# Attention and gated FFN on one core: k-v products moved into the runs of the batch before, remainder pairs two at a time

## The chip, the cores and the metric

The kernel runs on one core of a Trainium2 chip. A core has TensorE (PE), VectorE (DVE), ScalarE (ACT), GpSimd (POOL) and SyncE (SP), each with an instruction stream of its own, worked off in order, and 16 DMA engines that all of them share. PE writes its results to PSUM, which the kernel cuts into eight tiles of 128 x 512 numbers; DVE and ACT read them from there. SP issues no arithmetic here: its stream holds DMAs alone, and an instruction of SP that waits holds up all that stand behind it. POOL has arithmetic and DMAs in one stream. The metric is the device time of one execution in microseconds (us), as the median of several.

## The reference

For 8 batches, 8 heads, 576 positions and 64 dimensions:

```python
kv = np.einsum('bhsd,bhse->bhde', k, v)
out = np.einsum('bhsd,bhde->bhse', q, kv)
rms = np.sqrt(np.mean(out * out, axis=-1, keepdims=True) + 1e-06)
attn = out / rms * g_norm
x = attn.transpose(0, 2, 1, 3).reshape(4608, 512)
rms = np.sqrt(np.mean(x * x, axis=-1, keepdims=True) + 1e-06)
xn = x / rms * rms_g
g = xn @ w_gate                      # 512 x 1536
silu = g * (1.0 / (1.0 + np.exp(-g)))
result = (silu * (xn @ w_val)) @ w_out
```

So attention has no softmax: a batch needs one 64x64 product of k and v for each head, and then q times it ("o"). Both norms are folded into one factor for each position and head.

## The kernel before

**Work and groups.** A batch's 576 positions are cut into 512 main ones, four chunks of 128, and a remainder of 64. The FFN runs over nine groups of 512 rows: the main positions of batches 0 to 6 in order, then the eight remainders together (`xr`, the group that the code calls B), then batch 7. In a group, the FFN is a row of slots: 24 for the first layer, alternately a gate (4 matmuls of 128x512, then silu on ACT) and a value (4 matmuls, then their product with silu on DVE), and 16 slots of 3 matmuls for the second layer. The attention of batch b is spread over the slots of group b-1, so that its x is there when group b starts. "Group 1" below is the stretch in which the attention of batch 2 is made, and so on; slot numbers count from the group's start.

**Who sets the order.** `Placer` (line 40) is a planner: it holds a load for each engine and slot. `put` gives an operation to the first slot from a given one in which the engine's backlog, by the costs written in the code, stays under a bound (`ROOM` lists what a slot of a kind offers, `BEHIND` what backlog is allowed; POOL has 0.85 a slot in the first layer, 0.65 in the second, and 2.0 of backlog). What is put first takes the room; what is put later goes where room is left. Instructions come out slot by slot: first the slot's operations for engines other than PE, then the FFN's matmuls of the slot, then the slot's other PE work. DMAs on SP have a cost of zero, and a landing time that the planner assumes (6 slots for q, 4 for x). The waits themselves come from semaphores that the framework adds by data; the planner sets the order alone.

**A batch's attention** (`place_attention`, line 669). (1) k and v come by POOL's DMAs, which also convert them to bf16 (`loads_kv`: k main, k remainder, v main, v remainder; two buffers of each, by the parity of the batch). (2) q comes by SP into `stg`, is converted by POOL in two halves (`main_q`), its remainder apart (`remq`, one tile for two batches), and is then transposed by SP's DMAs (`qT_dma`, line 379). (3) PE makes the k-v products: 40 matmuls of 64x64 (`kv_mm`, line 285), into a PSUM tile that two DVE copies empty (`kv_half`). (4) PE makes o, 32 matmuls (`o_heads`, line 412). (5) ACT squares and copies o, POOL weights the squares with the norm's gain, DVE sums both, works out the factor in a chain of 13 small steps and multiplies (`xna`). (6) SP transposes the result into x in two DMAs (`x_dma`, line 645). In SP's order, the transposition of the next batch's q can stand ahead of x's.

**Runs.** Steps 3 and 4 put runs of small matmuls between those of the FFN. Batches 2 and 3 have a run of k-v products each; batches 4 and 5 share one, 6 and 7 too (`mate`). Each of these runs stands in the last slots of the group before the one in which o follows; o of a batch stands behind slot 2 of its group (batch 2: slot 7).

**Remainders.** The remainders' o is made for two batches at a time (16 matmuls, `o_rem`), with the o of batch 2 (remainders of 0 and 1), 3, 5 and 7. Its two PSUM tiles, half full, are squared and copied by ACT as four halves each. It is a fifth chunk of its batch for all that follows. The products of k and v lie in three tiles `kvs`, each a block-diagonal 128x128 for two heads, two of them cleared by POOL at the start.

PSUM is split into three tiles `mm1` for the FFN's first layer, two `o2` for the second, and three `att`; o of a batch takes both `o2`, two `att`, and, with a remainder, a third `att` and an `mm1`.

Of the kernel before, what the change touches and what calls it, by code (L numbers as in the profile page):

```python
# [87 lines left out]
def kernel(  # L88
# [38 lines left out]
    xna_p = pool("xna", 2)  # L127
    x_p = pool("x", 3)
# [30 lines left out]
    q01r = consts.tile([2 * REM, H, D], BF16, name="q01r")  # L159
# [29 lines left out]
    def load_cast(b, t, heads=None):  # L189
        to = qc if t == 0 else (vc if t == 2 else kc)[b % 2]  # L190
        if heads is None:
            if t == 0:
                to = q01r[b * REM : (b + 1) * REM]
            else:
                to = to[:REM, :, NC * D :]
            return nc.gpsimd.dma_start(
                out=to, in_=src[t][b, :, MAIN:S, :].rearrange("h p d -> p h d")
            )
        view = src[t][b, :, 0:MAIN, :].rearrange("h (p c) d -> p h (c d)", c=NC)[:, heads[0] : heads[1]]
        return nc.gpsimd.dma_start(out=to[:, heads[0] : heads[1], : NC * D], in_=view)  # L200
# [62 lines left out]
    class Att:  # L263
        def __init__(self, b):
            self.b = b
            self.kv, self.qT = kvs[b % 2 if b else 2], qTs[b % 2]
            self.chunks = NC + (b == 2 or b > 2 and b % 2)
            if b < 2:
                self.qTj = self.qT.rearrange("p c j t -> p (c j t)").rearrange("p (j c t) -> p j c t", j=NS, c=NC + 1)
# [51 lines left out]

        def kv_half(self, half):
            rows, cols = slice(half * D, (half + 1) * D), slice(half * D, (half + 1) * D)
            nc.vector.tensor_copy(out=self.kv[rows, :, half, :], in_=self.kv_ps[rows, :, cols])  # L324
# [54 lines left out]
        def qT_dma(self):  # L379
            flat = mains[self.b, 0].rearrange("p c h d -> p (c h d)")  # L380
            nc.sync.dma_start_transpose(out=self.qT[:, 0:NC].rearrange("p c j t -> p (c j) t"), in_=flat)
            if self.chunks > NC:
                rem = q01r if self.b == 2 else rems[0][self.b // 2 % 2]
                nc.sync.dma_start_transpose(out=self.qT[:, NC], in_=rem.rearrange("p h d -> p (h d)"))

        def o_rem(self):

            of = (kvs[2], kvs[1]) if self.b == 2 else (kvs[0], kvs[1])
            self.o[NC] = [
                pool_.tile([128, H // 2, D], FP32, name=name) for pool_, name in ((att_p, "att"), (mm1_p, "mm1"))  # L390
            ]
            for j in range(NS):
                for n in range(2):
                    at = slice(n * REM, (n + 1) * REM)
                    for half in range(2):
                        rows = slice(half * D, (half + 1) * D)
                        nc.tensor.matmul(  # L397
                            self.o[NC][half][at, j, :], lhsT=self.qTj[rows, j, NC, at],
                            rhs=of[n][rows, j, half, :], start=True, stop=True, skip_group_check=True,
                        )  # L400

        def sq_rem(self, half):
            if NC not in self.sq:
                self.sq[NC] = sq_p.tile([128, 2, H, D], BF16, name="sq")
            nc.scalar.activation(out=self.sq[NC][:, 0, half:H:2, :], in_=self.o[NC][half], func=ACT.Square)  # L405

        def outa_rem(self, half):
            if NC not in self.outa:
                self.outa[NC] = outa_p.tile([128, H, D], BF16, name="outa")
            nc.scalar.copy(out=self.outa[NC][:, half:H:2, :], in_=self.o[NC][half])  # L410

        def o_heads(self):
# [5 lines left out]
            for c in range(NC):  # L418
                for j in range(NS):
                    for half in range(2):  # L420
# [3 lines left out]
                            rhs=self.kv[rows, j, half, :], start=True, stop=True, skip_group_check=True,  # L424
# [4 lines left out]
        def part(self, t, n):  # L429

            if n >= NC:
                return t[:, n]
# [12 lines left out]
        def xna_pairs(self, o, js, c0, c1):  # L445
            if not hasattr(self, "xna"):
                self.xna = xna_p.tile([128, NC + 1, H, D], BF16, name="xna")
# [6 lines left out]
        def o_of(self, c):  # L454
            return self.o[c] if c >= NC else self.o["main", c].rearrange("p c h d -> p (c h) d")
# [60 lines left out]
        def red(self, c, which):  # L516
            if self.st is None:
                self.st = stat.tile([128, 2, NC + 1, H], FP32, name="st")
            of = self.sq[c][:, which]
            if c < NC:  # L520
                of = of.rearrange("p (c h) d -> p c h d", c=2)
            nc.vector.reduce_sum(out=self.part(self.st[:, which], c), in_=of, axis=AX.X)  # L522

        def chain_t(self):
            if not hasattr(self, "al"):
                t = lambda n, dt=FP32, h=H: stat.tile([128, NC + 1, h], dt, name=n)
                self.u, self.r, self.t, self.z, self.nt, self.al = (t(n) for n in ("u", "r", "t", "z", "nt", "al"))
                self.s = stat.tile([128, NC + 1], FP32, name="srow")
# [57 lines left out]
        def xna_(self, c, eng):  # L586
            if not hasattr(self, "xna"):
                self.xna = xna_p.tile([128, NC + 1, H, D], BF16, name="xna")
            if c < NC:
                of = self.o["main", c] if self.b == 1 else self.outa[c].rearrange("p (c h) d -> p c h d", c=2)  # L590
                return eng.tensor_tensor(  # L591
                    out=self.part(self.xna, c), in0=of,
                    in1=self.part(self.al, c).to_broadcast([128, 2, H // 2, D]), op=OP.mult,
                )
            return eng.tensor_tensor(
                out=self.xna[:, c], in0=self.outa[c], in1=self.al[:, c, :].to_broadcast([128, H, D]), op=OP.mult
# [48 lines left out]
        def x_dma(self, c0, c1):  # L645
# [3 lines left out]
            else:  # L649
                b = self.b // 2 * 2 if self.b > 2 else 0  # L650
                to = xr[:, :, b * REM : (b + 2) * REM]
                of = self.xna[:, NC].rearrange("p h d -> p (h d)")
# [16 lines left out]
    def place_attention(P, b, casts=(), at=0, chain_at=0, mate=None):  # L669
# [3 lines left out]
        N1 = range(a.chunks)  # L673
        P.floor = max(P.floor, at)
        load = P.put("SP", 0.0, a.qT_dma, casts[:1] if b == 2 else casts)
        qt = [("DMA", load[1] + QT_SLOTS)]
        if kv is None:
            of = [a] + ([Att(mate)] if mate else [])
            p = P.psum(1.2, lambda: [o.kv_mm(ALL) for o in of], casts, len(of))
            out_ = [[P.put("DVE", 0.4, lambda o=o, h=h: o.kv_half(h), [p]) for h in range(2)] for o in of]  # L680
            for tile_, ops in zip(P.tiles[-len(of) :], out_):
                tile_ += ops
            kv = out_[0]
            if mate:
                ahead[mate] = of[1], out_[1]
        else:
            P.floor = max(P.floor, start + 2)
        outs, reds = {}, []
        rem = a.chunks - NC
        main = P.psum(0.73 + 0.25 * rem, a.o_heads, kv + qt, 2 + rem)  # L690
        for c in (*N1[NC:], *N1[:NC]):
            if c == NC:
                for n in (1, 0):
                    s = P.put("ACT", 0.38, lambda n=n: a.sq_rem(n), [main])
                    outs[c] = P.put("ACT", 0.38, lambda n=n: a.outa_rem(n), [main])
                P.tiles[-1] += [s, outs[c]]
            else:
                s = P.put("ACT", 0.6, lambda c=c: a.sq_(c), [main])
                outs[c] = P.put("ACT", 0.6, lambda c=c: a.outa_(c), [main])
                if c >= 2:  # L700
                    P.tiles[c - NC - rem] += [s, outs[c]]
            assert outs[c][1] < start + 2 * NF, (b, outs)
            w = P.put("POOL", 1.2, lambda c=c: a.wsq(c, nc.gpsimd), [s])
            reds.append(P.put("DVE", 0.68, lambda c=c: a.red(c, 0), [s]))
# [424 lines left out]
```

## Time and profile before

| | us |
|---|---|
| median of three runs | 317.73 (317.66 to 317.91) |
| the profiled execution's own time | 317.42 |
| its span, first to last instruction | 315.6 |
| PE busy | 309.0 |
| DVE, ACT, POOL busy | 167.4, 139.0, 87.3 |
| FFN matmul, start to start | 0.216 |
| a slot of the first layer, of the second | 0.86, 0.65 |
| transposing DMA of q, issue to landing (median) | 7.5 |
| of x | 3.2 |
| a load of k, of v (512 KB, median) | 7.9, 12.8 |

The span is that of the profile's instructions; the time of an execution has some 1.8 us around it. In a line of a timeline stand the start, the length, the engine, the line of the kernel, the operation, what it writes and reads, and how many were merged; the first two are in us. Matmuls overlap: one of 512 columns is listed with 0.38 us, but the next starts 0.216 after it. Some matmul records are missing, so that a count can be one or two short. A line of a DMA issue gives the time from issue to landing at its end; q0 is the queue that POOL's loads go through, q1 that of SP's DMAs, and the last figure of a queue's line is the time that its packets took, as a share of the 16 engines (over 100% where packets overlap in an engine).

### The profile page before, as it was taken

Reading aid. Unit: us, or ns where it says so; the run is one execution under the profiler, and the core shown is the slowest. Engines: PE = TensorE matmul, PEld = TensorE weight load, DVE = VectorE, ACT = ScalarE, POOL = GpSimd, SP = SyncE. Lnnn points to the kernel's source line nnn. Section 1 sums busy time; section 2 is a strip of 40 time slices with the busy share of each in tenths; the row PEclk is TensorE's granted clock in tenths of the full one; section 3 lists DMA queues with packets and bytes.
Section 4 is the critical chain, followed back from the end, with each engine's and each line's share of the span. In section 5 each row is a group of like instructions: output and inputs, shape, how many; then the busy total and the mean of one; then the engine's idle time right before and its main releaser. Section 6 shows DMA issues by size and latency. Waiting matters only on the chain.

```text
span 315.6 us, 5661 instructions
## 1 busy us (share of the span) xinstructions
PE 309.0 (98%) x2187; PEld 154.4 (49%) x2208; DVE 167.4 (53%) x375; ACT 139.0 (44%) x261; POOL 87.3 (28%) x108
## 2 busy tenths in 40 slices
PE   8999999999999999999999999999999999999995
PEld 3688645544444445444444454444444444444443
DVE  5574455579669634854196638470868034103310
ACT  2474464595487324631483227323832233233321
POOL 8836430076068205730080007100600000000000
PEclk9999999999999999999999999999999999999999
DMA  8999999999799988998523444424001600140002
GB/s 202 198 201 199 196 236 201 175 234 164 181 172 210 166 185 125 249 173 172 169 69 67 100 134 136 83 59 141 3 0 35 184 0 0 30 104 1 2 33 100
DMA packets 78358, 40.18 MB, mean 127 GB/s; under 512 B 43000, under 2 KB 73852, under 8 KB 78332
## 3 DMA queue, kind: packets, MB, share of 16 engines
q0 software_dynamic: 32304, 14.75, 36.4%
q1 hardware_dynamic: 45328, 24.48, 32.0%
q10 hardware_dynamic: 700, 0.59, 0.6%
q8 instruction: 17, 0.28, 0.4%
q14 instruction: 9, 0.07, 0.1%
HBM read 37.78 MB, written 9.44 MB: 150 GB/s over the span
## 4 chain that ended last, share of the span: by engine, by line
PE 91%; DMA 3%; POOL 3%; issue 1%; DVE 0%; ACT 0%; POOLq 0%
PE mm L762 58%; PE o L811 27%; DMA wv<-in_moe_w_val_dram 3%; PE mm L811 2%; PE att L294 2%; POOL vc L200 1%; POOL main_q L208 1%; PE o L422 1%; PE att L422 1%; POOL wg L248 0%; PE mm L842 0%; PE o L842 0%; PE att L621 0%; DVE h L783 0%; PE att L397 0%
## 5 line engine op out<-in xcount | busy, mean ns | idle before, releaser
L783 DVE TENSOR_TENSOR h<-silu,mm 128x512 bf16<-128x512 bf16 (+1 forms) x114 | 73.9, 649 | 101.5 <-PE mm L762 92.8
L771 ACT ACTIVATE silu<-mm 128x512 bf16<-128x512 f32 (+1 forms) x115 | 65.1, 570 | 83.5 <-PE mm L762 73.1
L762 PE MATMUL mm<-x,wv 128*128 128x512 bf16 (+1 forms) x405 | 97.6, 364 | 0.3
L762 PE MATMUL mm<-x,wg 128*128 128x512 bf16 (+1 forms) x401 | 97.1, 364 | 0.4 <-ACT silu L771 0.2
L811 PE MATMUL o<-wo,h 128*128 128x512 bf16 x385 | 87.9, 379 | 0.7 <-issue 0.3
L762 PEld LDWEIGHTS <-wv 128*128 128x128 bf16 x468 | 45.0, 98 | 46.5 <-DMA wv<-in_moe_w_val_dram 0.4
L762 PEld LDWEIGHTS <-wg 128*128 128x128 bf16 x456 | 44.3, 98 | 47.5 <-issue 0.4
L811 PEld LDWEIGHTS <-h 128*128 128x128 bf16 x420 | 40.6, 98 | 47.6
L514 POOL TENSOR_TENSOR sq<-sq,g 128x512 bf16<-128x512 bf16 x28 | 32.0, 1154 | 98.4 <-ACT sq L405 66.8
L831 ACT COPY osb<-o 128x512 f32<-128x512 f32 x33 | 19.2, 586 | 68.7 <-PE o L811 65.8
L522 DVE TENSOR_REDUCE st<-sq 128x8 f32<-128x512 bf16 x56 | 35.9, 678 | 0.0
L591 DVE TENSOR_TENSOR xna<-outa,al 128x512 bf16<-128x512 bf16 x24 | 15.1, 686 | 0.0
L324 DVE CAST kvs<-att 64x256 bf16<-64x256 f32 x14 | 5.9, 422 | 16.8 <-PE att L294 16.6
L200 POOL DMA_DIRECT2D kc<-in_k_dram x7 | 6.5, 922 | 29.0 <-PE att L294 26.1
L762 PE MATMUL mm<-xr,wv 128*128 128x512 bf16 x47 | 12.3, 379 | 0.1
L762 PE MATMUL mm<-xr,wg 128*128 128x512 bf16 x47 | 12.3, 379 | 0.1
L229 POOL CAST main_q<-stg 128x1024 bf16<-128x1024 f32 x10 | 10.1, 1044 | 1.3 <-DMA stg<-in_q_dram 1.3
L931 ACT ACTIVATE wv<-wv,gain 128x384 bf16<-128x384 bf16 x16 | 9.0, 608 | 0.4 <-PE mm L762 0.4
L200 POOL DMA_DIRECT2D vc<-in_v_dram x10 | 8.6, 860 | 2.1 <-PE mm L762 1.1
L258 PE MATMUL mm<-idle 128*128 128x512 bf16 x19 | 7.0, 541 | 1.3 <-DVE idle L138 1.2
L811 PE MATMUL mm<-wo,h 128*128 128x512 bf16 x23 | 7.4, 380 | 0.2 <-issue 0.2
L459 ACT ACTIVATE sq<-att 128x512 bf16<-128x512 f32 x12 | 7.5, 629 | 0.0
(151 smaller groups left out, 189.6 us busy)
## 6 DMA issues: line engine op xcount, KB each, us to landing
out_dram<-osb SPq DMA_DIRECT2D x27, 256.0 KB, 2.5
stg<-in_q_dram SPq DMA_DIRECT2D x6, 1024.0 KB, 10.8
vc<-in_v_dram POOLq DMA_DIRECT2D x7, 512.0 KB, 12.8
kc<-in_k_dram POOLq DMA_DIRECT2D x7, 512.0 KB, 7.9
out_dram<-osb SPq DMA_DIRECT2D x17, 128.0 KB, 2.4
wg<-in_moe_w_gate_dram POOLq DMA_DIRECT2D x4, 384.0 KB, 10.6
wv<-in_moe_w_val_dram POOLq DMA_DIRECT2D x4, 384.0 KB, 11.8
wo<-in_moe_w_out_dram POOLq DMA_DIRECT2D x4, 384.0 KB, 14.5
```

Of the source, the lines that this page charges most:

```text
L200: return nc.gpsimd.dma_start(out=to[:, heads[0] : heads[1], : NC * D], in_=view)
L229: return copy(out=mains[b, t][:, cs[0] : cs[1], h0:h1, :], in_=staged[b, t].rearrange("p h (c d) -> p c h d", c=NC)[:, cs[0] : cs[1], h0:h ...
L459: nc.scalar.activation(out=self.sq[c][:, 0], in_=self.o_of(c), func=ACT.Square)
L514: eng.tensor_tensor(out=self.sq[c][:, 1], in0=self.sq[c][:, 0], in1=g2, op=OP.mult)
L522: nc.vector.reduce_sum(out=self.part(self.st[:, which], c), in_=of, axis=AX.X)
L591: return eng.tensor_tensor(out=self.part(self.xna, c), in0=of, in1=self.part(self.al, c).to_broadcast([128, 2, H // 2, D]), op=OP.mult,)
L762: nc.tensor.matmul(ps[:, : c1 - c0], lhsT=w[n][:, s, jj * 128 : (jj + 1) * 128], rhs=x_of(g, s, c0, c1), start=s == 0, stop=s == NS - 1)
L771: nc.scalar.activation(out=sis[g, j][:, c0:c1], in_=ps, func=ACT.Silu)
L783: nc.vector.tensor_tensor(out=hs[g, j][:, c0:c1], in0=sis[g, j][:, c0:c1], in1=v_ps, op=OP.mult)
L811: nc.tensor.matmul(ps, lhsT=hs[g, j][:, t * 128 : (t + 1) * 128], rhs=wo[j // OB][:, j % OB, :], start=j == 0, stop=j == NF - 1)
L831: (eng.copy if eng is nc.scalar else eng.tensor_copy)(out=o, in_=ps)
L931: A.mul(out=w[:, s], in_=w[:, s], mul=gain[:, s : s + 1])
```

## The change

- The k-v products of batch 4 move behind o of batch 3 in the same run, those of 5 behind o of 4, those of 6 and 7 behind o of 5 (`mates` in place of `mate`); the second mate's products go to an `mm1` tile. Batches 2 and 3 keep their runs of products, now with a planned cost of 0.85 in place of 1.2.
- Each batch has a tile of products of its own; for batches 2 to 7 it holds the 64x64 products alone, without the zero blocks. One clearing on POOL goes.
- The remainders' o is made with batch 6 (remainders of 0 to 3) and batch 7 (4 to 7), two pairs at a time, in two full PSUM tiles that are squared, copied, weighted and summed like those of the main chunks. The factors of the remainder are a chain of their own, behind the main one in batch 6 and ahead of it in batch 7. q's remainders are transposed where they were, into tiles of their own (`qTr`).
- The loads of k and v for batch 4 move from slot 14 of group 2 to slot 20 of group 1, and are given to the planner before all else of that group but the loads of batch 3. The other loads stay where they were.

```diff
+    rna_p = pool("rna", 1)
...
-    kvs = [consts.tile([128, NS, 2, D], BF16, name=f"kvs{n}") for n in range(3)]
-    qTs = [consts.tile([128, NC + 1, NS, 128], BF16, name=f"qTs{n}") for n in range(2)]
+    kvs = [consts.tile([128, NS, 2, D] if n < 2 else [128, NS, D], BF16, name=f"kvs{n}") for n in range(B)]
+    qTs = [consts.tile([128, NC, NS, 128], BF16, name=f"qTs{n}") for n in range(2)]
+    qTr = [consts.tile([128, NS, 128], BF16, name=f"qTr{n}") for n in range(B // 2)]
...
-            self.kv, self.qT = kvs[b % 2 if b else 2], qTs[b % 2]
-            self.chunks = NC + (b == 2 or b > 2 and b % 2)
+            self.kv, self.qT = kvs[b], qTs[b % 2]
+            self.rems = {6: (0, 1), 7: (2, 3)}.get(b, ())
+            self.chunks = NC + len(self.rems)
...
-        def kv_mm(self, js):
+        def kv_mm(self, js, pool=None):
             if not hasattr(self, "kv_ps"):
-                self.kv_ps = att_p.tile([128, NS, 2 * D], FP32, name="att")
+                self.kv_ps = (pool or att_p).tile([128, NS, 2 * D], FP32, name="mm1" if pool is mm1_p else "att")
...
-            if self.chunks > NC:
-                rem = q01r if self.b == 2 else rems[0][self.b // 2 % 2]
-                nc.sync.dma_start_transpose(out=self.qT[:, NC], in_=rem.rearrange("p h d -> p (h d)"))
+            n = {2: 0, 3: 1, 5: 2, 7: 3}.get(self.b)
+            if n is not None:
+                rem = rems[0][n % 2]
+                nc.sync.dma_start_transpose(out=qTr[n], in_=rem.rearrange("p h d -> p (h d)"))
...
+            for half, (pool_, name) in enumerate(((att_p, "att"), (mm1_p, "mm1"))):
+                self.o["main", NC + half] = pool_.tile([128, 2, H // 2, D], FP32, name=name)
+            for i, r in enumerate(self.rems):
+                for j in range(NS):
+                    for n in range(2):
+                        at = slice(n * REM, (n + 1) * REM)
+                        for half in range(2):
+                            rows = slice(half * D, (half + 1) * D)
+                            nc.tensor.matmul(
+                                self.o["main", NC + half][at, i, j, :], lhsT=qTr[r][rows, j, at],
+                                rhs=Att(2 * r + n).kv_of(rows, j, half), start=True, stop=True, skip_group_check=True,
+                            )
...
-    def place_attention(P, b, casts=(), at=0, chain_at=0, mate=None):
+    def place_attention(P, b, casts=(), at=0, chain_at=0, mates=()):
...
+        def products():
+            a.o_heads()
+            for o, pool_ in zip(of, (None, mm1_p)):
+                o.kv_mm(ALL, pool_)
+
+        base = len(P.tiles)
+        main = P.psum(0.73 + 0.25 * len(a.rems) + 0.65 * len(of), products, kv + qt, 2 + rem + bool(of))
+        for n in reversed(range(len(of))):
+            ahead[mates[n]] = of[n], halves(of[n], main)
+            if n == 0:
+                P.tiles[-1] += ahead[mates[n]][1]
+        for c in (*reversed(range(NC, a.chunks)), *range(NC)):
+            s = P.put("ACT", 0.6, lambda c=c: a.sq_(c), [main])
+            outs[c] = P.put("ACT", 0.6, lambda c=c: a.outa_(c), [main])
...
+        for c0, c1 in (rests, mains) if b == B - 1 else (mains, rests)[: 1 + rem]:
+            prev = [r for c in range(c0, c1) for r in reds[c]]
+            for n in range(0, 13, 4):
+                prev = [P.put("DVE", 0.8, lambda n=n, c0=c0, c1=c1: [f() for f in a.chain(c0, c1)[n : n + 4]], prev, chain_at)]
...
-    G.memset(kvs[0], 0.0)
     G.memset(kvs[1], 0.0)
...
         if b == 2:
             for n, f in enumerate(loads_kv(b + 1)):
                 P.at("POOL", 0.85, f, starts[1] + 11 + n)
+            for f in loads_kv(b + 2):
+                P.put("POOL", 0.85, f, at=starts[1] + 20)
...
-            end = place_attention(P, b, casts, s0 - 2, s0 + 2 * NF - 4, b + 1 if b in (4, 6) else None)
+            end = place_attention(P, b, casts, s0 - 2, s0 + 2 * NF - 4, {3: (4,), 4: (5,), 5: (6, 7)}.get(b, ()))
...
             casts = place_casts(P, b + 1, starts[b - 1] + 18)
-            for of, at in {3: ((5, 0), (4, 14)), 4: ((6, 0), (7, 14))}.get(b, ()):
+            for of, at in {3: ((5, 0),), 4: ((6, 0), (7, 14))}.get(b, ()):
                 for f in loads_kv(of):
                     P.put("POOL", 0.85, f, at=starts[b - 1] + at)
```

More of the change, by code (lines that the diff above doesn't have):

```diff
@@ L386, in o_rem @@
         def o_rem(self):
[L388 to L400, printed above, removed]
@@ L423, in o_heads @@
                             self.o["main", c // 2 * 2 + half][:, c % 2, j, :], lhsT=self.qTj[rows, j, c, :],
-                            rhs=self.kv[rows, j, half, :], start=True, stop=True, skip_group_check=True,
+                            rhs=self.kv_of(rows, j, half), start=True, stop=True, skip_group_check=True,
                         )
@@ L676, in place_attention, with halves @@
         qt = [("DMA", load[1] + QT_SLOTS)]
+        def halves(o, p):
+            return [P.put("DVE", 0.4, lambda o=o, h=h: o.kv_half(h), [p]) for h in range(2)]
         if kv is None:
[L678 to L682, printed above, removed]
@@ L683, in place_attention @@
-            kv = out_[0]
-            if mate:
-                ahead[mate] = of[1], out_[1]
+            p = P.psum(0.85, lambda: a.kv_mm(ALL), casts)
+            kv = halves(a, p)
+            P.tiles[-1] += kv
         else:
             P.floor = max(P.floor, start + 2)
[L688 to L701, printed above, removed]
+        outs, reds = {}, {}
@@ L713, in place_second @@
+        return ends[NC if b == B - 1 else 2] + X_SLOTS
     def place_second(P, s):
```

76 lines of the change are left out of this document (34 added, 42 removed).

## The prediction

> **What bounds the kernel now.** I read the page first, then the chain in order of time, then POOL's, SP's and the DMA queues' views of the stretch in which the change puts new work.
>
> ```profile
> PE 309.0 (98%) x2187; PEld 154.4 (49%) x2208; DVE 167.4 (53%) x375; ACT 139.0 (44%) x261; POOL 87.3 (28%) x108
> ...
> PE 91%; DMA 3%; POOL 3%; issue 1%; DVE 0%; ACT 0%; POOLq 0%
> ```
>
> PE is the bound, and after the start (a weight load ends at 20.74 us) it practically never waits: the chain is a row of matmuls 0.216 us apart (12 of L762 in 2.59 us). So only two things can move the end: the PE time of the short runs between the FFN's matmuls, and a new PE wait. PE's timeline around two such runs:
>
> ```profile
> 57.06 1.03 PE L762 MATMUL mm<-x,wg 128*128 128x512 bf16 x4
> 58.02 0.82 PE L294 MATMUL att<-vc,kc 128*64 128x64 bf16 x40
> 58.77 0.39 PE L762 MATMUL mm<-x,wv 128*128 128x512 bf16 x1
> ...
> 122.77 0.81 PE L762 MATMUL mm<-x,wg 128*128 128x512 bf16 x3
> 123.52 0.41 PE L422 MATMUL o<-kvs,qTs 64*128 64x64 bf16 x16
> 123.76 0.40 PE L422 MATMUL att<-kvs,qTs 64*128 64x64 bf16 x16
> 124.09 0.82 PE L762 MATMUL mm<-x,wv 128*128 128x512 bf16 x3
> ```
>
> The next FFN matmul was due at 57.06+4x0.216=57.92 and came at 58.77: 40 k-v products cost 0.85 us, of which 0.09 is the way in and 0.11 the way out. Likewise o alone costs 124.09-123.42=0.67; with one remainder pair (run at 61.47) 0.92, so a pair is 0.25, of which about 0.12 is the switch of matmul shape (o's last starts near 61.92, the pair's first at 62.04); 80 products (118.78) cost 1.48, since the weights of the next FFN matmul load at 120.17 instead of 118.69.
>
> **PE's runs, part by part.** Removed: two runs of 80 products (-2.96). Added: 40 products behind o of batches 3 and 4, 80 behind o of 5, without a way in but with a switch of shape. No row has o followed by these products; the nearest is the run at 38.00, turned q (64*64) and then these very products: last turn near 38.52, first product 38.64, so 0.12. A group of 40 is then 0.12+0.63=0.75, of 80 0.12+1.26=1.38, together 2.88. Remainder pairs: four of 0.25 go (-1.00); two groups of two pairs come, the second pair 16 steps of 0.0084 without a switch: 2x(0.25+0.13)=+0.76. Sum 2.88-2.96+0.76-1.00 = **-0.32 us**. Bounds: a switch that costs nothing gives -0.32-3x0.10=-0.6; one as dear as a whole way in and out (0.20), and one more between the two pairs (2x0.12), gives about +0.2. I take 0.12, the row with the same second shape.
>
> **Work off PE.** ACT trades 16 half-size squares and copies (0.37 to 0.40 each) for 8 full ones (0.60): -1.3 us. DVE gets two more chains of 13 small steps (rows 0.17 to 0.25, about 2.5 us each) in batches 6 and 7, where it is busy 18.8 of 34 us (183 to 217). The k-v copies (14 of 0.42) stay. Batch 7's second tile and the double remainder sit in the FFN's mm1 buffers: its two copies, or a square and a copy (0.2+2x0.6=1.4 us), are over before that buffer's turn comes again, two slots (1.73 us) later. If that 0.3 us of cover went, PE would wait by the excess, three times at most. POOL loses a 0.55 us memset at 23.64; nothing waits for it. The remainders' transposes of q and x stay four each. All this is zero on PE.
>
> **The moved load.** Batch 4's four k, v loads leave POOL's place behind batch 3's weighted squares (99.28) for slot 20 of group 1. The planner gives them room there first (three in slot 20, one in 21, at 0.85 each against 0.85 of room and a lag of 2.0); the first half of batch 3's q cast still fits in slot 18, the second goes to slot 22 and the remainder's cast to 23, behind the loads. And SP is in order: transposing batch 3's q waits for those casts, and batch 2's x behind it on SP, although its turn comes only at slots 27 and 29. Group 2's first matmul needs all of that x. So I followed POOL and SP:
>
> ```profile
> 66.03 0.95 POOL L200 DMA_DIRECT2D kc<-in_k_dram  x1
> 66.98 0.69 POOL L196 DMA_DIRECT2D kc<-in_k_dram  x1
> ...
> 70.42 3.39 POOL L514 TENSOR_TENSOR sq<-sq,g 128x512 bf16<-128x512 bf16 x3
> 73.74 2.01 POOL L229 CAST main_q<-stg 128x1024 bf16<-128x1024 f32 x2
> 75.71 0.60 POOL L236 CAST remq<-rstg 128x512 bf16<-128x512 f32 x1
> ```
> ```profile
> 75.78 1.86 SPq L381 DMA_TRANSPOSE qTs<-main_q  x1
> 77.75 1.75 SPq L384 DMA_TRANSPOSE qTs<-remq  x1
> ...
> 83.14 1.29 SPq L653 DMA_TRANSPOSE x<-xna  x1
> ...
> 104.52 5.05 SPq L381 DMA_TRANSPOSE qTs<-main_q  x1
> ...
> 136.85 4.68 SPq L381 DMA_TRANSPOSE qTs<-main_q  x1
> 141.64 1.20 SPq L384 DMA_TRANSPOSE qTs<-remq  x1
> ```
>
> Before: POOL works without a pause from 64.94 until the remainder's cast ends at 76.31; x's second transpose starts at 83.14 and lands 3.3 us later, 86.4; group 2's first matmul starts at 87.33. Cover: 0.9 us.
>
> After, step by step. (1) POOL: four loads more, 0.95+0.69+0.94+0.69=3.27; less one weighted square (1.1) that is gone and one (1.1) done earlier, in POOL's idle time before 64.9, as o of batch 2 comes a slot sooner (the planner charges 0.85 for 40 products and 0.73 for o, where it charged 1.2 and 0.98): the cast ends at 76.31+1.07=77.4. (2) The DMAs: batch 3's loads land by 76.4 (69.72+6.7). Batch 4's, issued at 72.4 to 75.7, queue behind. The nearest row is the same four loads issued at 99.28 behind batch 5's (landed 89.51+13.8=103.3): v landed at 100.89+8.7=109.6, 6.3 later. So v lands at 76.4+6.3=82.7; by the load at 131.96 (9.4 us) 83.5, by that at 68.78 (7.3) 81.4. (3) SP: q's transpose issued into such loads holds SP until v has landed: 104.52+5.05=109.57 against 109.6, and 136.85+4.68=141.53 against 131.96+9.4=141.4. Without them it holds SP 1.86. The queues show why:
>
> ```profile
> q0 software_dynamic: 1503, 0.56, 157.2%
> issues: line engine op xcount, KB each, median us to landing
> qTs<-main_q SPq DMA_TRANSPOSE x1, 8.0
> ```
>
> This is 104.5 to 107.5: SP's transposes (q1) move no packet for 3 us. So SP is free at 82.7. (4) Remainder's transpose 1.25 (row 141.64), x's first 1.28, a store 0.6: x's second starts at 85.9 and lands 3.3 later, at **89.2**. (5) PE is there at 87.33-0.25 (no pair in o of batch 2) = 87.08. It waits **2.1 to 2.2 us**, where it waited none before. By the bounds of (2) x lands between 87.9 and 90.0, a wait of 0.8 to 2.9.
>
> Other moves: batch 6's loads no longer wait 15.4 us on POOL for PE; they go right behind batch 4's q cast, between 101.3 and 104.5 (its end now, less the 3.2 of loads that leave its place), and its transpose may hold SP some 8 us, to 112; x of batch 3 is DVE's then (113.98 now, landing by 117.3, wanted at 121.0). Some 3.5 us of cover.
>
> Sum: -0.32+2.17 = +1.85 on the profiled execution's 317.42 (span 315.6 and 1.8 around it), 319.3. The median of the runs is 0.31 above that execution: **319.6**.
>
> **Rivals.** *Hidden anyway, not slower (0.15):* loads and transposes share the engines, SP is free after 1.9 us as at 75.78, x's second starts near 82.9 and lands at 86.2, before 87.08: 317.4. It decides when SP is free before 80.6 (87.08 less 6.5). The window above, and the one of 136 to 139 (q0 alone too), speak against it. The Trainium skill's page "DMA: Bandwidth & Descriptors", section on queues, rings and completion order, says that each DMA engine round-robins between the queues it has work for, packet by packet. By that rule q1 could not stand still, and the time would be this rival's; the trace disagrees (no q1 packet in 3 us).
>
> *A longer wait (0.10):* x's last transpose (85.9) meets batch 5's loads, which POOL issues when batch 3's products end, 87.02 before. q's load issued at 88.53 moved no packet until after 91.0 while they ran, 2.5 us. Then 322.1. Against it: x's is issued before them.
>
> *The clock (0.04):* a PE wait could drop the granted clock; it is 1.00 throughout, and only the start shows slow matmuls: the 17 of L258 from 1.20 on take 6.4 us, where 17x0.216 is 3.7. One more such spell adds about 2.6: 322.2. The Trainium skill's page "TensorE: Matmul & The Clock Gate", Part 1, puts the drop at an idle window of about 3.4 us. The forecast wait stays below it, and no run here has shown one.
>
> **How the numbers follow.** The wait as worked out 0.68, hidden 0.15, longer 0.10, clock 0.04, others 0.03. A difference of 0.2% (0.6 us) is about what a measurement of this kernel tells from none. Slower: 0.68, 0.10, 0.04 and part of the others, 0.83; same: most of the hidden case and very short waits, 0.14; faster needs -0.64, the end of the runs' bound: 0.03. The main case spans 318.2 to 320.4 (wait 0.8 to 2.9), with the runs' bounds 317.9 to 320.9; with the hidden case 317.3, and up to 321.5 for some of the longer ones.
>
> **What would show it.** Right: PE idle about 2 us just before group 2's first L762 near 87, ended by x's transpose; q's transpose near 77 holding SP some 5 us; eight short runs from 57 on, 0.3 us less in sum. Wrong: x landing before 87, or PE idle in groups 5 and 6 behind ACT or DVE.

## The result and the profile after

The changed kernel took **320.87 us** in the median (319.02 to 322.10), the kernel before 317.81 (317.57 to 318.25) on the same chip: a ratio of 1.0084, 95% interval 1.0063 to 1.0104. On another occasion it took 319.57 us in the median of seven executions against 317.69; two of the seven, of 327.46 and 330.65 us with mean clocks of 0.988 and 0.979, are far slower than the rest and not in the comparison, and no trace of them exists. The other five have a median of 319.20, and a ratio of 1.0055 (1.0032 to 1.0078). The changed kernel is slower, by 0.3% to 1.0%.

The profiled execution took 321.32 us with a span of 319.5, the fifth of its six in order. Its page, with the lines that answer to those of before (engines, the granted clock in 40 slices, the shares of the chain):

```profile
PE 311.0 (97%) x2208; PEld 155.2 (49%) x2208; DVE 172.6 (54%) x399; ACT 138.2 (43%) x253; POOL 87.1 (27%) x107
...
PEclk9799999999999999999999999999999999999999
...
PE 88%; DMA 3%; SPq 3%; POOL 2%; DVE 1%; issue 1%; ACT 1%; DVEq 0%; POOLq 0%
```

PE is still most of the chain, but SP, which had no share before, now has 3%. The 7 in the clock's row, at 8 to 16 us, is the lead; it is a matter of its own, below. First the view that the prediction was about, the waits of PE, summed by line and releaser:

```profile
PE mm L762 <- DMA x<-xna: 1.7, 1, 1.7
...
PE mm L314 <- DMA vc<-in_v_dram: 1.1, 2, 0.8
```

and PE's timeline around the first of them, with the next run of small matmuls:

```profile
88.71 0.82 PE L811 MATMUL o<-wo,h 128*128 128x512 bf16 x3
91.28 1.04 PE L762 MATMUL mm<-x,wg 128*128 128x512 bf16 x4 [1.75 <-DMA x<-xna]
...
93.11 0.41 PE L418 MATMUL o<-kvs,qTs 64*128 64x64 bf16 x16
...
93.68 0.82 PE L296 MATMUL att<-vc,kc 128*64 128x64 bf16 x40
94.43 1.04 PE L762 MATMUL mm<-x,wg 128*128 128x512 bf16 x4
```

Group 2's first matmul was due at 88.71 + 3 x 0.216 = 89.36 and started at 91.28: a wait of 1.92 us, counted from start to start. The chain in order of time, cut to the steps before it (start, length, what), says where it comes from:

```profile
76.19 0.88 POOL vc L201
77.07 0.69 POOL vc L197
77.75 1.05 POOL main_q L230
78.80 0.56 POOL remq L237
79.36 5.06 SPq L387
...
85.82 1.26 SPq L643
...
87.80 3.43 DMA x<-xna
...
91.28 1.90 PE mm L762 x8
```

Batch 4's v loads, batch 3's casts behind them on POOL, q's transpose on SP, then x's. The DMA queues from 78.9 to 82, while that transpose (`qTs<-main_q`) stood on SP:

```profile
q0 software_dynamic: 1474, 0.54, 151.0%
...
issues: line engine op xcount, KB each, median us to landing
qTs<-main_q SPq DMA_TRANSPOSE x1
```

POOL's loads (q0) moved 1474 packets, SP's queue q1 none. SP was free again at 84.4, when batch 4's v was landing (84.97).

**The sum of this execution.** Its span is 3.9 us longer than before's 315.6. Group 1 started at 55.68 instead of 53.61, +2.07. From there to the start of group 2: 35.60 us instead of 33.72, +1.88 (a wait of 1.92, 0.2 of a small one told below, less the 0.25 of batch 2's remainder pair). From there to the start of the last group, 193.52 instead of 193.61, -0.09. Of the 2.07, the lead, the change is not the cause: the first v load landed at 9.48 instead of 8.29, PE waited 0.8 us for it and 0.35 for a later part of v, and PE's clock then stood at half from 11.58 to 14.99. The same kernel, profiled again, started group 1 at 53.91. From group 1 on the change costs 1.88 - 0.09 = 1.79 us, against a forecast of 1.85.

### The profile page after: what moved, and what is told of

It is laid out like the page before. It is cut to its first block, busy times and chain, and to the rows that moved or that the text cites. A ratio compares the mean times of both kernels' runs of the same rounds, so it can differ in the third digit from the quotient of the medians.

```text
span 319.5 us, 5698 instructions
## 1 busy us (share of the span) xinstructions
PE 311.0 (97%) x2208; PEld 155.2 (49%) x2208; DVE 172.6 (54%) x399; ACT 138.2 (43%) x253; POOL 87.1 (27%) x107
## 4 chain that ended last, share of the span: by engine, by line
PE 88%; DMA 3%; SPq 3%; POOL 2%; DVE 1%; issue 1%; ACT 1%; DVEq 0%; POOLq 0%
PE mm L762 56%; PE o L811 24%; DMA vc<-in_v_dram 2%; PE mm L811 2%; SPq L387 2%; PE att L296 1%; DMA x<-xna 1%; PE o L418 1%; PE att L418 1%; POOL vc L201 1%; PE att L466 0%; PE mm L314 0%; DVE xna L443 0%; PE mm L842 0%; PE o L842 0%
## 5 line engine op out<-in xcount | busy, mean ns | idle before, releaser
L811 PE MATMUL o<-wo,h 128*128 128x512 bf16 x396 | 89.4, 379 | 0.0
L330 DVE CAST kvs<-att 64x256 bf16<-64x256 f32 x12 | 5.1, 422 | 7.3 <-PE att L296 7.2
L453 ACT ACTIVATE sq<-att 128x512 bf16<-128x512 f32 x14 | 8.7, 620 | 0.0
L457 ACT CAST outa<-att 128x512 bf16<-128x512 f32 x14 | 8.5, 606 | 0.0
```

What stands on the lines that cost most here:

```text
L453: nc.scalar.activation(out=self.sq[c][:, 0], in_=self.o_of(c), func=ACT.Square)
L811: nc.tensor.matmul(ps, lhsT=hs[g, j][:, t * 128 : (t + 1) * 128], rhs=wo[j // OB][:, j % OB, :], start=j == 0, stop=j == NF - 1)
```

## The experiments

### Batch 4's products left alone

```diff
-            for f in loads_kv(b + 2):
-                P.put("POOL", 0.85, f, at=starts[1] + 20)
...
-            end = place_attention(P, b, casts, s0 - 2, s0 + 2 * NF - 4, {3: (4,), 4: (5,), 5: (6, 7)}.get(b, ()))
+            end = place_attention(P, b, casts, s0 - 2, s0 + 2 * NF - 4, {4: (5,), 5: (6, 7)}.get(b, ()))
...
-            for of, at in {3: ((5, 0),), 4: ((6, 0), (7, 14))}.get(b, ()):
+            for of, at in {3: ((5, 0), (4, 14)), 4: ((6, 0), (7, 14))}.get(b, ()):
```

> The change, but batch 4's products keep their own run at the end of group 2 and its loads their old place at slot 14 of group 2. My theory: no wait at the start of group 2; of the runs' -0.32 some 0.10 is given back (0.85 for a run of its own against 0.75 behind o): -0.2 us, 317.6. If the remainders or the other merged products cost PE anything, a wait shows in groups 5 or 6. If the change's start is slower for a reason of its own, up to 319.7.

Measured: 317.68 us against 317.96, ratio 0.9991 (0.9980 to 1.0001). A second set was to tell whether that is a gain:

> The variant in which batch 4's products and loads stay where they were, once more, to see whether it beats the kernel before: from the runs' lengths 0.3 us less than before, 317.4 against 317.7; if its first gain was chance, within 0.1 us of before.

Measured: 317.84 against 317.86, ratio 0.9999 (0.9990 to 1.0008). No wait of PE for x is listed; the longest are

```profile
PE mm L259 <- DVE idle L139: 1.2, 1, 1.2
PE o L611 <- DVE xna L443: 0.2, 1, 0.2
```

of which the first, in the lead, is in every trace. So all of the loss hangs on batch 4's products and their loads; without them the rest of the change is neither a loss nor a gain that can be told. From group 1 to the last group this kernel takes 227.10 us, before 227.33; the 0.23 is there in the trace, and it is below what the times can show.

### Batch 4's loads earlier, or made small

```diff
-                P.put("POOL", 0.85, f, at=starts[1] + 20)
+                P.put("POOL", 0.85, f, at=starts[1] + 5)
```

> The change, with batch 4's four loads issued from slot 5 of group 1 (right behind batch 2's products) instead of slot 20, so that they land before batch 3's q is transposed. My theory (the loads' traffic holds SP, and batch 2's x lands late): q's transpose holds SP under 2.5 us, x's second transpose lands before 86.5, PE does not wait at the start of group 2, and what is left is the shorter runs, -0.3 us: 317.5. If the wait came from anything else in the change, it stays near 2 us: 319.5 or more. The start, up to 21 us, is the same as the change's; if the change itself makes the start slower (2.1 us in its profiled execution), that shows here too: up to 319.6.

Measured: 319.69 against 317.96, ratio 1.0059 (1.0044 to 1.0074). The expectation failed. SP's timeline:

```profile
66.14 1.65 SPq L223 DMA_DIRECT2D rstg<-in_q_dram  x1
78.30 4.68 SPq L387 DMA_TRANSPOSE qTs<-main_q  x1
83.08 1.21 SPq L391 DMA_TRANSPOSE qTr<-remq  x1
...
85.01 2.65 SPq L643 DMA_TRANSPOSE x<-xna  x2
```

Batch 4's loads, issued from 59.36 to 61.85, were out of the way, but batch 3's v loads (landed 82.61 and 83.16) and the loads of batch 3's q (issued at 65.47, and at 66.14 for the remainder, which landed at 78.4) then queued behind them. POOL's cast waited 4.5 us for q, q's transpose was issued at 78.30, and PE waited 1.8 us. So an earlier slot alone doesn't help: half a megabyte each of k and v more has still to land before x, whichever batch's loads come last. The next kernel takes that traffic away and leaves every instruction in place; it loads one head of eight of batch 4's main k and v and leaves the other seven out:

```diff
-        return [lambda t=t, hs=hs: load_cast(b, t, hs) for t in (1, 2) for hs in ((0, H), None)]
+        return [lambda t=t, hs=hs: load_cast(b, t, hs) for t in (1, 2) for hs in ((0, 1 if b == 4 else H), None)]
```

> The change, with each of the two main loads of batch 4 cut to one head of eight, so that batch 4's result is wrong from the other seven heads' old data; POOL issues the same four DMAs at the same place. My theory: POOL's casts end as late as in the change (3 us later than before), but the traffic is gone, q's transpose holds SP about 1.9 instead of 5.6 us, x lands about 3.5 us earlier, and the wait of 1.9 falls to under 0.5. Rival (POOL's order alone): the wait stays near 1.9.

Measured: 318.76 against 317.96, ratio 1.0023 (1.0006 to 1.0040). At group 2 the wait was gone: q's transpose held SP for 2.92 us instead of 5.59 (1.9 was expected), and x's second was issued at 83.02. But the profiled execution, at 321.90 the slowest of eleven, had another one, at group 3:

```profile
76.36 2.92 SPq L387 DMA_TRANSPOSE qTs<-main_q  x1
...
115.82 4.91 PE L811 MATMUL o<-wo,h 128*128 128x512 bf16 x22
122.72 1.37 PE L762 MATMUL mm<-x,wg 128*128 128x512 bf16 x4 [1.99 <-DMA x<-xna]
```

Batch 6's loads, which before waited on POOL for PE until 119.88, went out from 104.69 to 107.19 and landed from 114.92 to 121.12. x of batch 3, issued at 112.85 and 114.81, landed at 121.33 and 122.68, 8 us after its issue instead of 3.3. PE had wanted it at 115.82 + 22 x 0.216 = 120.57, so it waited 2.15 us (the 2.36 of the next expectation counts from the start of the last matmul). The same edit for batches 4 and 6:

> The changed kernel in which the main loads of k and v of batches 4 and 6 carry one head of eight (seven eighths of those two batches' k and v aren't loaded; every instruction stays). With batch 4's loads alone cut, the wait at group 2 was gone, but PE waited 2.36 us at group 3 for x of batch 3 behind batch 6's loads, and the median was 318.8. Theory (each of the two moved sets of loads can hold one x): no PE wait of 0.5 us at groups 2 or 3, a time of 317.4 to 317.8, that is before - 0.3. Rival (the second wait is of the merged runs or of DVE, not of the loads): it stays, 318.5 to 319.

Measured: 317.94 against 317.69, ratio 1.0008 (0.9999 to 1.0016). No wait for x in groups 2 and 3, as the theory had it, and the time is that of before; it is 0.1 above the range expected; PE waited 0.6 us for DVE once in group 1 (more on that below). In the changed kernel itself the second wait doesn't appear: group 2, already late, gives x of batch 3 time (landed 121.85, wanted at 123.8).

### Is it POOL's order, SP's order or the traffic?

The casts ahead of batch 4's loads on POOL:

```diff
-            for f in loads_kv(b + 2):
-                P.put("POOL", 0.85, f, at=starts[1] + 20)
...
             casts = place_casts(P, b + 1, starts[b - 1] + 18)
+            if b == 2:
+                for f in loads_kv(4):
+                    P.put("POOL", 0.85, f, at=starts[1] + 20)
```

> The change, with batch 3's q casts given to the planner ahead of batch 4's loads, so that POOL casts first and then loads; same traffic. My theory: q's transposes get ahead of the loads, but batch 2's x now meets them: its first or second transpose is held until batch 4's v has landed (about 86), so x's second lands near 89 to 90 and PE still waits 1 to 3 us. Rival (POOL's order alone): q's transpose starts 3 us earlier, x lands by 85, no wait: 317.5.

Measured: 323.29 against 317.96, ratio 1.0183 (1.0157 to 1.0209), the worst of the kernels with the whole change. SP:

```profile
73.89 3.29 SPq L387 DMA_TRANSPOSE qTs<-main_q  x1
77.28 1.85 SPq L391 DMA_TRANSPOSE qTr<-remq  x1
79.65 1.80 SPq L643 DMA_TRANSPOSE x<-xna  x1
...
82.18 3.98 SPq L643 DMA_TRANSPOSE x<-xna  x1
```

q's transpose came 3 us earlier, as the edit wants it (73.89; 77.04 in the second profile of the changed kernel), and x's first nearly 5 us earlier (79.65 and 84.32); but x's two transposes now stood among batch 4's loads themselves (landed 83.74 to 90.77) and landed 9.6 and 9.3 us after their issue. PE waited 4.14 us (due 87.43, first matmul 91.57). POOL's order alone is not the cause. The other order, on SP, x ahead of q:

```diff
-        load = P.put("SP", 0.0, a.qT_dma, casts[:1] if b == 2 else casts)
+        load = P.put("SP", 0.0, a.qT_dma, casts[:1] if b == 2 else casts, starts[b - 2] + 30 if b in (3, 4) else 0)
```

> The changed kernel with one order on SP turned: the transposes of q of batches 3 and 4 come behind both transposes of x of the batch before, not ahead of them. The loads stay where the change put them. Theory (x waits on SP behind a transpose of q that itself stands behind batch 4's loads): x's first transpose of batch 2 is then issued near 81.5, held until v has landed (82.9, or 84.2 with the remainder's), the second lands at 86.0 to 87.8, against PE's 87.3: a wait of 0 to 0.6 us, and q's transposes end at 89 to 91, in time for o at 91; the time 317.5 to 318.3. Rival (SP's order doesn't matter, since the loads hold every transpose alike, as where the casts came ahead of the loads and x landed 4.3 us late): 319.5 to 321.

Measured: 317.57 against 317.69, ratio 1.0001 (0.9991 to 1.0012). SP and PE:

```profile
80.53 1.27 SPq L643 DMA_TRANSPOSE x<-xna  x1
...
82.52 1.30 SPq L643 DMA_TRANSPOSE x<-xna  x1
83.92 3.14 SPq L387 DMA_TRANSPOSE qTs<-main_q  x1
87.15 1.22 SPq L391 DMA_TRANSPOSE qTr<-remq  x1
```
```profile
86.87 0.82 PE L811 MATMUL o<-wo,h 128*128 128x512 bf16 x3
87.53 1.03 PE L762 MATMUL mm<-x,wg 128*128 128x512 bf16 x4
```

x landed at 86.47, inside the 86.0 to 87.8 expected, and PE didn't wait. One detail was wrong: the issue of x's first transpose did not hold SP until v had landed. It took 1.27 us while v's loads were on their way (landed 83.33 and 83.87), although q1 moved only 32 packets until 82. So the order on SP settles the loss: the loads may stay where the change put them. Like the kernel in which batch 4's products are left alone, this one is not faster than before by anything that can be told.

### The changed kernel again, and the clock

> The changed kernel once more. In the first profile of it two things are mixed: the wait of 1.93 us ahead of group 2, which the theory puts down to batch 4's loads, and a lead that ended 2.07 us late (group 1 at 55.84, where five other traces have 53.8 to 54.1), which the theory puts down to chance in that one execution, by way of a late first v load and 3.41 us at half clock. If so, here group 1 starts near 54.0, PE still waits 1.9 to 2.2 us near 87, and an execution without any clock drop takes 317.4 - 0.3 + 2.0 = 319.1, one with a drop of 3.41 us (1.7 us of work lost) 320.8; the median of all 319.3 to 321. Rival, that the change itself makes the lead late: group 1 at about 55.8 again.

Measured: 319.57 (above). Group 1 began at 53.91, so the first profile's late lead was its own. PE's wait came, a little longer than the 1.9 to 2.2 us expected; then something more. PE, and the windows around it (length; busy us and matmuls of PE, then of its loads, DVE, ACT, POOL; granted clock; DMA share; GB/s):

```profile
86.92 0.82 PE L811 MATMUL o<-wo,h 128*128 128x512 bf16 x3
89.85 1.89 PE L762 MATMUL mm<-x,wg 128*128 128x512 bf16 x4 [2.11 <-DMA x<-xna]
91.53 1.06 PE L762 MATMUL mm<-x,wv 128*128 128x512 bf16 x2
```
```profile
86.23:89.65 3.42, 1.51 (x44) 0.85 (x43) 1.39 (x4) 1.10 (x2) 2.39 (x3) 1.00 1.01 232
89.65:93.06 3.41, 3.21 (x8) 1.04 (x8) 0.00 (x0) 1.29 (x3) 0.75 (x2) 0.50 0.90 191
93.06:100.00 6.94, 6.94 (x99) 3.71 (x99) 5.76 (x11) 5.26 (x11) 3.04 (x3) 1.00 1.31 253
```

The wait is 2.28 us (due 87.57). Then eight matmuls take the time of sixteen: from 89.65 to 93.06 the clock is at half. Group 2 lasts 34.09 us instead of 32.52 with the same work at full clock (the kernel with x ahead of q), so this costs 1.57 us. The sum against before: lead +0.30, group 1 +2.22, group 2 +0.59, the rest +0.89, together the 4.0 us of the span (319.6 - 315.6). Group 2 without the half clock is 0.98 shorter than before, since products that had a run at its end now stand in later groups, and the 0.89 of the rest is these.

All changes of the clock in the traces stand whole multiples of 3.41 us apart within an execution, and where the raster begins differs from one execution to the next. Half a clock came in the window behind one in which PE was busy for 0.44 of the time (here), 0.42 (small loads for batch 4, 119.87 to 123.29), 0.34 (casts first, 89.33 to 92.74) or 0.07 and less (the kernels with the move alone, below); it did not come behind 0.49 (casts first, 85.91 to 89.33), 0.56 (earlier loads, a wait of 1.8) or 0.65 (the change's first profile, whose wait lay across two windows). The half clock of that profile's lead stands behind a window of 0.66, among other shapes of matmul, and doesn't fit this boundary. The ends of the executions do, where PE runs out of work: windows of 0.18 (x ahead of q), 0.21 and 0.38 (the change's two profiles) are followed by half clock, 0.61 (before) and 0.66 (small loads for batch 4) are not.

By the mean clocks, this is what makes the change's times wide. The four executions of 321.3 to 322.1 us have mean clocks of 0.993 or 0.994, as a drop of 3.41 us gives; the seven of 318.8 to 320.4 have 0.998 to 1.000. In one of the four, the first profile, the drop was the lead's; in the second profile it followed the wait for x; for the other two, which have no trace, the cause isn't shown.

The Trainium skill's page "TensorE: Matmul & The Clock Gate", Part 1, has a free-running window of 3413 ns and half clock after an idle window of about 3.4 us. The traces agree on the window; they disagree on "idle": 1.51 us of matmuls within the window did not keep the clock up.

### The move of the loads alone

The kernel before with this step of the change; the bound that the planner sets on the end of batch 2's attention is a slot wider:

```diff
+            for f in loads_kv(b + 2):
+                P.put("POOL", 0.85, f, at=starts[1] + 20)
...
-            assert end < starts[b] + (b == 1), (b, end, starts)
+            assert end < starts[b] + (b < 3), (b, end, starts)
...
-            for of, at in {3: ((5, 0), (4, 14)), 4: ((6, 0), (7, 14))}.get(b, ()):
+            for of, at in {3: ((5, 0),), 4: ((6, 0), (7, 14))}.get(b, ()):
```

> The kernel before with one step of the change alone: batch 4's four k, v loads go to slot 20 of group 1; all products and remainder pairs stay in runs of their own. Theory (the moved loads are all of the loss): PE waits about 2 us ahead of group 2, ended by x's second transpose, and the time is 317.9 + 2.0 = 319.9, up to 321.5 where a clock drop follows; some 0.3 us slower than the whole change. Rival (the merged runs cost, through DVE, ACT or the buffers, and the load is beside the point): within 0.3 us of 317.9.

Measured: 328.85 against 317.69, ratio 1.0347 (1.0324 to 1.0370). Both theories missed: the move alone costs 11 us, far more than the whole change. The wider bound tells it beforehand: by the planner's own count batch 2's attention ends in the very slot in which group 2 starts, against 4 slots ahead of it in the kernel before and 7 in the changed one. PE:

```profile
87.47 0.60 PE L811 MATMUL o<-wo,h 128*128 128x512 bf16 x2
96.88 1.89 PE L762 MATMUL mm<-x,wg 128*128 128x512 bf16 x4 [8.81 <-DMA x<-xna]
98.56 1.91 PE L762 MATMUL mm<-x,wv 128*128 128x512 bf16 x4
```

A wait of 8.8 us, and half clock from 92.63 to 102.87, three windows. x's second transpose was issued at 88.48, behind batch 5's first load (87.81, issued once the products of batch 3 free its buffer). The first guess was that q's transposes ahead of x on SP made it so late:

> The move of batch 4's loads alone, with q's transposes of batches 3 and 4 behind x's on SP. The move alone took 328.9 us: x's second transpose was issued at 88.48, behind batch 5's first load (87.81), and landed after 96. Theory (that place on SP is all of it): x's second transpose is issued at 82.5 to 85, lands before 88, PE waits at most 0.5 us ahead of group 2, no half clock, 317.7 to 318.4. Rival (the move costs by itself, in POOL's order of casts and squares): a wait of 2 us or more, 319.7 or above.

Measured: 328.43 against 317.86, ratio 1.0348 (1.0304 to 1.0392). Wrong again: x's second was issued at 88.44 and PE waited 10.9 us. The edit did not turn the order either: it keeps q's transposes from coming before slot 30, the planner has this x later than that, and on SP q's still came first. So the theory was not tested by it. But the trace of the move alone answers it: DVE finished x's last chunk at 87.49, so no order on SP could have had x's second transpose issued by 85. POOL and DVE of the move alone show why x is so late:

```profile
73.42 0.95 POOL L200 DMA_DIRECT2D kc<-in_k_dram  x1
...
75.91 0.71 POOL L196 DMA_DIRECT2D vc<-in_v_dram  x1
76.61 1.19 POOL L514 TENSOR_TENSOR sq<-sq,g 128x512 bf16<-128x512 bf16 x1
```
```profile
77.78 2.71 DVE L933 TENSOR_SCALAR wg<-wg,gain 128x384 bf16<-128x384 bf16 x3
80.41 0.67 DVE L522 TENSOR_REDUCE st<-sq 128x8 f32<-128x512 bf16 x1
...
85.60 1.89 DVE L591 TENSOR_TENSOR xna<-outa,al 128x512 bf16<-128x512 bf16 x3
```

In the kernel before, o of batch 2 has a fifth chunk, the remainders. Its weighted square now stands behind batch 4's loads and ends at 77.8 (before at 73.8); DVE has just begun 2.7 us of folding gains, the factors come at 84, and x's last chunk at 87.5. In the changed kernel batch 2 has no fifth chunk, so the chain is done earlier, and x is issued at 84.32 and 86.48 in the second profile, 0.8 us ahead of batch 5's first load (87.26). Whether the late place behind batch 5's loads makes the difference between 2 and 9 us, the last kernel tells (the edit is against the move alone):

```diff
-            for of, at in {3: ((5, 0),), 4: ((6, 0), (7, 14))}.get(b, ()):
+            for of, at in {3: ((5, 10),), 4: ((6, 0), (7, 14))}.get(b, ()):
```

> The move of batch 4's loads alone, with batch 5's loads put ten slots later (behind four of batch 3's weighted squares, so that POOL issues them near 99 instead of 87.8). In both runs with the move alone x's second transpose was issued at 88.44 to 88.48, 0.7 to 0.9 us behind batch 5's first load, and PE waited 8.8 and 10.9 us. Theory (two causes one behind the other: the fifth weighted square behind batch 4's loads makes x ready only at 87.8, and batch 5's loads, then ahead of it, hold the transpose): x is still issued near 88.5, lands 3.3 later at 91.8, PE waits 3.8 to 4.2 us from 87.9 or so, one to two windows at half clock follow (1.7 each): 322.5 to 325. Rival (batch 5's loads are beside the point; the transpose is slow by batch 4's loads or by itself): a wait of 8 us or more and 327.5 to 331.

Measured: 323.44 against 317.90, ratio 1.0170 (1.0146 to 1.0194). x was issued at 88.56 and PE went on at 91.93, a wait of 3.86 us (due 88.07), with one window at half clock:

```profile
91.93 1.89 PE L762 MATMUL mm<-x,wg 128*128 128x512 bf16 x4 [3.69 <-DMA x<-xna]
```

All of that is as expected, though batch 5's loads went out at 104.18 and not near 99. So 5 to 7 us of the move's wait, taken between single profiled executions, are batch 5's loads ahead of x's last transpose, and the rest is the lateness of x. One thing in it is not explained: between 88.6 and 92 of the move alone, DMA engines stood idle for parts of the time while the transpose didn't land.

## Why the prediction was right

**The runs (-0.32).** Measured -0.315: the eight runs, from their first weight load to that of the next FFN matmul, sum to 8.58 us, the ten of before to 8.71, and two ways in (0.093 each) are saved. (The lower bound took 0.10 for a switch that the text puts at 0.12; with 0.12 it is -0.7, and nothing hangs on it.) The switch from o to products cost 0.12 to 0.15, the row taken; o with 40 products is 1.33 us, o with two pairs 0.95. In the kernel with x ahead of q, 0.15 us of it is left from group 1 on; the rest goes in the small wait told next.

**The wait (+2.17).** The steps, with the first profile's times less the 2.07 us of its late lead: the casts end at 77.28 (forecast 77.4), SP is free at 82.35 (82.7), x's second transpose is issued at 85.73 (85.9) and lands at 89.16 (89.2); PE was due at 87.29 (87.08). The wait was 1.92 and, in the second profile, 2.28. The chain of steps (1) to (5) holds, and the runs show that its links are needed: without the loads' bytes, or with x ahead of q on SP, no wait is left. The rule within step (3), that q's transpose holds SP until v has landed, doesn't: SP was free 0.55 us before v landed in the first profile (84.42 and 84.97) and 1.7 before in the second (82.42 and 84.15), and x's first transpose, where it came ahead, was not held at all. What ends the hold is not shown.

**The work off PE.** Taken as zero on PE, and no trace shows PE waiting for ACT or DVE in groups 5 and 6. One small wait was not foreseen: with the loads in group 1, one second-layer weight load waits 0.5 us for DVE's h (0.8 with the loads earlier, 1.0 and 1.1 with small loads), and PE loses 0.2 to 0.7. Without the move it doesn't, nor with the casts ahead of the loads on POOL. DVE and POOL in the second profile:

```profile
76.25 0.82 DVE L572 SCALAR_TENSOR_TENSOR al<-nt,y 128x32 f32<-128x32 f32 x1
77.10 0.51 DVE L570 TENSOR_TENSOR nt<-al 128x32 f32<-128x32 f32 x1
```
```profile
75.93 1.08 POOL L230 CAST main_q<-stg 128x1024 bf16<-128x1024 f32 x1
```

The two DVE steps take 0.18 and 0.19 in the kernel without the move, where POOL's casts are over by 74.3; here they lie beside the second cast, which the loads pushed back, and beside that of the remainder (76.91 to 77.56), each ends 0.05 or 0.06 after the cast beside it, and the h behind them is late.

The other move, batch 6's loads, was given 3.5 us of cover for x of batch 3. It had less: x landed 1.95 us ahead of PE, in a group 2 that had itself been put back by 1.9 us. With the wait of group 2 gone that cover is gone too, as one of the runs showed.

**The rivals.** "Hidden anyway" by sharing of the engines did not come: q1 moved nothing for 3 us. By the Trainium skill's page "DMA: Bandwidth & Descriptors", section on queues, rings and completion order, each engine takes its queues in turn, packet by packet; the 1474 packets against none are not like that. But other stretches are: from 92 to 96 of the move alone q0 moved 1140 packets and q1 1068. Whether q1 had any packet to move in the 3 us isn't shown, so these runs show that the transpose came late and don't show by which rule. "A longer wait", x's last transpose behind batch 5's loads, is real, but not in the two profiles of the change, of which the second escaped it by 0.8 us: it is the case of the move alone, and its price was mis-sized, 9 to 11 us of wait with three windows or more of half clock in place of 2.5. The two executions of the change of 327.46 and 330.65 us, with mean clocks of 0.988 and 0.979, are like those of the move alone (327.82 to 330.21, 0.983 to 0.990) and may be this case too; without a trace that isn't shown.

**The clock** is the step that failed. In the prediction it is a rival with 0.04, on the argument that the forecast wait stays below 3.4 us, and the sum has nothing for it. A wait of 2.28 us was followed by half clock, since 2.08 of it fell into one window, and 4 of 11 executions have the low mean clock, one of them through the lead. The price, put at 2.6, is at most 1.7 for a window (1.57 measured). The forecast median of 319.6 is near that of the executions without a drop (seven, median 319.20); the first set, with three of six below 0.995, lies 1.3 above it. That the second set's median of all seven is 319.57 is luck: two executions that the prediction doesn't account for lift it.

## What to carry to other kernels

When a load is moved forward, ask which transfers of other queues stand behind it until it has landed, and put the one that PE needs first ahead of them in its own queue: here one order on SP made the same loads free. A part of a change can cost far more alone than within it (11 us against 2 to 3), here because another part took away the work that would have stood behind it; try parts alone before adding up their prices. On an engine that never pauses, a wait of 2 us may be charged once more through the clock, by where it falls.

## What the runs showed of the hardware

- The granted clock changes in a raster of 3.41 us whose start differs between executions. After the lead, half clock followed windows in which PE was busy for 0.44 or less, and full clock stayed at 0.49 and more; in one lead it followed a window of 0.66. A window at half cost 1.57 us. In the move alone, the window of 0.75 in which PE restarted, at half clock, was followed by another at half, the next, of 1.00, by full clock.
- Some steps of DVE on 128x32 numbers, 0.18 to 0.19 us elsewhere, took 0.51 to 0.95 while POOL converted q. Not every step did (one beside the remainder's cast kept 0.19 in the kernel with batch 4's products left alone), and with the small loads one took 0.81 to 0.84 beside POOL's issues of loads; no run varied this by itself.
- x's two transposes land each 3.0 to 3.5 us after the issue in a quiet queue, 9.3 to 9.6 among POOL's loads, and take SP between 1.2 and 4.0 us to issue.
